# Second batch: keys and values before queries, query chunks straight into the numerator, and a later value load for the third batch

## The chip, the cores and the metric

The kernel runs on one core of a Trainium2 chip. The metric is the device time of one execution in microseconds (us). A core has a matrix engine (PE in the profile; PEld is its weight load), a vector engine (DVE), an activation engine (ACT), a general engine (POOL) and a queue engine (SP) that issues most DMAs; 16 DMA engines move the data.

## The reference

For 8 batches with 8 heads, 576 tokens and head dimension 64, a linear attention is computed, then a token-and-channel mixer on its output:

```python
def phi(x, c, s):
    r = np.maximum(x, 0.0)
    return np.concatenate([r * c, r * s], axis=-1)
q_p = phi(q, cos_w, sin_w)
k_p = phi(k, cos_w, sin_w)
kv = np.einsum('bhsf,bhsd->bhfd', k_p, v)
z = np.sum(k_p, axis=2)
num = np.einsum('bhsf,bhfd->bhsd', q_p, kv)
den = np.einsum('bhsf,bhf->bhs', q_p, z)[..., None] + 1e-06
x = num / den                      # heads side by side: 576 x 512
h = np.maximum(x.T @ w_tok1, 0.0) @ w_tok2
u = x + h.T
out = u + np.maximum(u @ w_ch1, 0.0) @ w_ch2
```

## The kernel before

Each batch's 576 tokens are cut into four chunks of 128 (`ci` 0 to 3) and a tail of 64 (`ci = R = 4`). The tails of two neighbouring batches share one 128-row tile. A batch has a **front** (class `Front`: attention and token mixer) and a **channel** part (class `Channel`: the two large matrix products). The front of batch b+1 is woven into the channel part of batch b.

The pieces of a front are: `feature`, called by `k_side` (KS) and `q_side` (QS), the ReLU features of keys and queries, a cosine and a sine half, on DVE (a sine half of the keys may go to ACT); `values` (V), the cast of the values into `v_aug`, which has a column of ones behind each head; `kv` (KV), eight matmuls of 128x65 for each chunk into one PSUM tile that collects all five chunks; `kv_out`, the copy of it to `kv_sb`, half on ACT, half on DVE; `q_trans` (QT), eight PE transposes of the query features into PSUM and a copy to `qpT`; `q_trans_dma`, the same by a transposing DMA from SP (batches 2 to 7); `num` (N), eight matmuls of `qpT` with `kv_sb`, then on DVE `den` (two small instructions) and a multiplication that gives the chunk of `x`; `mix_head` and `mix_tail`, the first token product `b_ps` and its ReLU `B`; `tok2` (T), the second token product `u_ps`, the addition on DVE that gives `u`, and a cast on ACT to `u_bf` or, for the tail, `ub_tail`; `u_trans_dma` and `tail_trans_dma`, transposing DMAs that give `uT` and `uT_tail`, which the channel part of the batch reads.

The channel part is a list of steps: 12 `c_step`s (C = 0; one 128-column block `c_ps` of the hidden layer each, four matmuls of 128x512, its ReLU `h1T` on ACT; for odd batches also four 128x128 matmuls `ct_ps` for the tails), and from step O = 12 on `o_step`s of two matmuls each (`o_ps`), whose sum with `u` goes to `o_sb` on DVE and out through SP. In the channel part of batch 0 the first twelve o steps run over chunks 0 and 1 together, four hidden blocks at a time, so that they need the three pieces of `w_ch2` one after the other.

`pieces` writes the weave as a plan of (slot, function, arguments); what stands at slot i is issued right after step i. Nothing reorders it: each engine runs its instructions in the order in which the program issues them. So the plan is the order on every engine and on SP's and POOL's DMA queues. PSUM has two pools: `ps_mm` with four one-bank buffers (`c_ps`, `ct_ps`, `o_ps`, `u_ps`, `b_ps`, half-width `qT_ps`) and `ps_at` with two two-bank buffers (`kv_ps`, `num_ps`, full-width `qT_ps`, some `u_ps`).

Batch 0 has a front of its own (`first_front`), in which nothing is woven. It ends with the first steps of channel 0. The front of batch 1 (`first` in `pieces`) is woven into channel 0, together with `tok2` of batch 0 (`u` in the plan). It has its own plan because its data arrive while it runs: `load_batch(1, ...)` waits for the first half of `w_ch1`. Later batches are loaded a batch ahead, by `load_batch` calls in the loop over steps at the end.

Of the kernel before, what the change touches and what calls it, by code (L numbers as in the profile page):

```python
# [10 lines left out]
BF16 = mybir.dt.bfloat16  # L11
# [5 lines left out]
def kernel(  # L17
# [15 lines left out]
    nc = tc.nc  # L33

    B, H, S, D = q.shape
# [4 lines left out]
    P = 128  # L40
    R = S // P
# [5 lines left out]
    NCH = D_ch // P  # L47
    HH = H // 2
# [6 lines left out]
    ORDER = (0, 1, 2, R, 3)  # L55
# [134 lines left out]
                in_=moe_w_ch1[ki * P:(ki + 2) * P, c2 * C2:(c2 + 1) * C2]  # L190
                .rearrange("(n c) d -> c n d", c=P)))
    after(w_ch1_done[0], k_done)
    def load_w_ch2(behind):
        done = [nc.gpsimd.dma_start(
            out=w_ch2[:, ki:ki + 4, :],
            in_=moe_w_ch2[ki * P:(ki + 4) * P, :].rearrange("(n t) d -> t n d", t=P))
            for ki in range(0, NCH, 4)]
        after(done[0], behind)
        return done

# [16 lines left out]
    class Front:  # L217
# [115 lines left out]
                     self.kv_ps[g][:, 0:HH * DP]  # L333
                     .rearrange("p (j d) -> p j d", d=DP)[:, :, 0:D1])

        def q_trans(self, ci, heads=(0, H), eng=nc.scalar):
            lo, hi = heads
            if hi - lo == H:
                qT_ps = ps_at.tile([P, H, P], BF16, name="qT_ps", tag="at")
            else:  # L340
                qT_ps = ps_mm.tile([P, HH, P], BF16, name="qT_ps", tag="mm")
            for h in range(lo, hi):
                nc.tensor.transpose(qT_ps[:, h - lo, :],
                                    self.q_of(ci)[:, h, :, :].rearrange("p a b -> p (a b)"), ident)
            dst = self.qpT[:, ci * H + lo:ci * H + hi, :] if ci < R else self.tail.qpT[:, lo:hi, :]
            if eng is nc.scalar:
                nc.scalar.copy(dst, qT_ps)
            else:
                nc.vector.tensor_copy(dst, qT_ps)  # L349
# [44 lines left out]
        def tok2(self, ci, pool=None, turn=True):  # L394
            res, tail = self.res, self.tail
            if ci == 0:
                res["u"] = keep.tile([P, R, Dm], F32, name="u_sb")
                if turn:
                    self.new_uT()
                    self.ub = once.tile([P, R, Dm], BF16, name="u_bf")  # L400
            if ci == R and not hasattr(tail, "u"):
                tail.new_u()
            if pool is None:
                u_ps = ps_mm.tile([P, Dm], F32, name="u_ps", tag="mm")
            else:
                u_ps = pool.tile([P, Dm], F32, name="u_ps", tag="at")
            rows = self.rows_of(ci)
            for ki in range(NT):
                nc.tensor.matmul(u_ps, w_tok2[:, ki, ci * P:(ci + 1) * P],  # L409
                                 self.B1[:, ki, :], start=(ki == 0), stop=(ki == NT - 1))  # L410
            u = res["u"][:, ci, :] if ci < R else tail.u[rows]
            nc.vector.tensor_add(u, u_ps[rows], self.x_of(ci)[rows])  # L412
            if ci == R:
                nc.scalar.copy(tail.ub[rows], u)
            elif turn:
                nc.scalar.copy(self.ub[:, ci, :], u)  # L416

        def new_uT(self):

# [41 lines left out]
        def pieces(self, b, before):  # L461


            first, odd = b == 1, b % 2 == 1
            V, KV, N = self.values, self.kv, self.num
            KS, QS, QT, T = self.k_side, self.q_side, self.q_trans, self.tok2
            C, O = 0, NCH
            if first:

                dve, every, u = nc.vector, (0, H), before.tok2  # L470
# [148 lines left out]
    def first_front(f):  # L619
# [13 lines left out]
                f.q_trans(ci, heads)  # L633
                busy(idle_ps, 1)
        f.q_side(R)
        f.q_trans(R)
        busy(idle_ps, 2)
        for ci in range(R):
            f.feature("k", ci, 0)
# [75 lines left out]


    results = [dict() for _ in range(B)]
    done = load_batch(1, "kqv", behind=w_ch1_done[1])
    w_ch2_done = load_w_ch2(done[1])
    tails = {0: tail0}  # L720
    f = Front(0, results[0], tail0)
    c = first_front(f)
    for b in range(B):
# [9 lines left out]
        for i, step in enumerate(c.steps(AHEAD if b == 0 else 0)):  # L733
# [46 lines left out]
```

## Time and profile before

| | |
|---|---|
| median of 3 runs | 276.12 us (275.65 to 276.5) |
| profiled execution | 274.87 us |
| its span in the trace | 273.1 us |
| PE busy | 260.9 us (96%) |
| DVE busy | 167.5 us (61%) |
| ACT busy | 127.0 us (47%) |
| POOL busy | 12.9 us (5%) |
| chain that ended last | PE 80%, DVE 11%, DMA 7% |

The span runs from the first to the last instruction; what the execution takes beyond it is starting and ending. Busy times of engines overlap. Matmuls are pipelined: a 128x512 matmul lasts 0.38 us in the records, and the next one starts sooner than that, so a busy PE is not a measure of how densely it is fed; the starts are.

### The profile page before, as it was taken

To read this page: it belongs to the slowest core of one execution; us is meant where nothing else is said; L and a number is where in the kernel's file an instruction comes from. 1 tells how busy PE (TensorE), PEld (TensorE's weight loads), DVE (VectorE), ACT (ScalarE), POOL (GpSimd) and SP (SyncE) were. 2 spreads that over 40 slices of the span, in tenths; PEclk is the share of its full clock that TensorE was granted. 3 is DMA by queue.
4 is the path that set the end of the run, shared out by engine and by line. 5 is a ranking of instruction groups with operands and counts; after the bars stand their busy time and mean duration, and the time that the engine had idled before them with its cause. 6 is when DMAs were issued, how large, how long until landed. Compare 5 with 4: busy or idle time off the path is not lost.

```text
span 273.1 us, 5108 instructions
## 1 busy us (share of the span) xinstructions
PE 260.9 (96%) x2029; PEld 139.3 (51%) x2050; DVE 167.5 (61%) x377; ACT 127.0 (47%) x225; POOL 12.9 (5%) x26
## 2 busy tenths in 40 slices
PE   7989979999899998999999999999999999999994
PEld 3665445446554454445654455446644455445543
DVE  6973698773876386559566387559466477720022
ACT  4955961068415184156615184338516273426500
POOL 6400240000000000000000000000000000000000
PEclk9999999999999999999999999999999999999999
DMA  7999999749985997947992969759993452170032
GB/s 224 338 270 275 333 175 276 252 98 282 272 257 183 244 212 182 333 117 234 218 305 77 264 201 253 246 149 273 157 321 105 135 95 61 41 192 21 2 99 93
DMA packets 91815, 53.68 MB, mean 197 GB/s; under 512 B 59408, under 2 KB 86928, under 8 KB 91792
## 3 DMA queue, kind: packets, MB, share of 16 engines
q1 hardware_dynamic: 88432, 49.62, 65.4%
q0 software_dynamic: 2832, 3.21, 7.0%
q10 hardware_dynamic: 528, 0.52, 0.6%
q8 instruction: 16, 0.26, 0.4%
q14 instruction: 7, 0.06, 0.1%
HBM read 35.85 MB, written 9.44 MB: 166 GB/s over the span
## 4 chain that ended last, share of the span: by engine, by line
PE 80%; DVE 11%; DMA 7%; issue 1%; DVEq 0%
PE o_ps L562 32%; PE c_ps L529 22%; PE b_ps L385 6%; PE u_ps L409 6%; DVE qp L264 4%; DMA qpT<-qp 4%; PE ct_ps L549 4%; PE num_ps L362 3%; PE kv_ps L321 3%; DVE x_sb L372 2%; DMA qt<-in_q_dram 2%; DMA uT<-u_bf 1%; DVE kp L264 1%; PE idle_ps L205 1%; PE c_ps L539 1%
## 5 line engine op out<-in xcount | busy, mean ns | idle before, releaser
L562 PE MATMUL o_ps<-w_ch,h1T 128*128 128x512 bf16 (+1 forms) x382 | 93.1, 372 | 0.6
L529 PE MATMUL c_ps<-uT,w_ch 128*128 128x512 bf16 (+2 forms) x384 | 91.9, 372 | 0.5 <-DMA uT<-u_bf 0.4
L533 ACT ACTIVATE h1T<-c_ps 128x512 bf16<-128x512 f32 x93 | 55.5, 598 | 60.2 <-PE c_ps L529 60.0
L562 PEld LDWEIGHTS <-h1T 128*128 128x128 bf16 x396 | 37.4, 98 | 39.7 <-issue 0.2
L529 PEld LDWEIGHTS <-w_ch 128*128 128x128 bf16 x384 | 33.2, 97 | 29.8 <-DMA uT<-u_bf 0.9
L567 DVE TENSOR_TENSOR o_sb<-o_ps,u_sb 128x512 f32<-128x512 f32 (+1 forms) x33 | 22.3, 674 | 37.1 <-PE o_ps L562 37.0
L412 DVE TENSOR_TENSOR u_sb<-u_ps,x_sb 128x512 f32<-128x512 f32 x32 | 22.0, 690 | 7.4 <-PE u_ps L409 6.7
L416 ACT CAST u_bf<-u_sb 128x512 bf16<-128x512 f32 x28 | 17.3, 618 | 16.9 <-DVE u_sb L412 15.2
L409 PE MATMUL u_ps<-B,w_tok 128*128 128x512 bf16 x77 | 21.9, 379 | 0.3
L390 ACT ACTIVATE B<-b_ps 128x512 bf16<-128x512 f32 x8 | 4.8, 597 | 36.0 <-PE b_ps L385 36.0
L372 DVE TENSOR_TENSOR x_sb<-num_ps,den 128x512 bf16<-128x512 f32 x28 | 19.4, 691 | 1.0
L264 DVE TENSOR_SCALAR qp<-qt,cos_t 128x512 bf16<-128x512 f32 (+1 forms) x35 | 16.7, 476 | 4.7 <-DMA qt<-in_q_dram 4.7
L549 PEld LDWEIGHTS <-w_ch 128*128 128x128 bf16 x192 | 14.0, 98 | 9.2
L385 PE MATMUL b_ps<-x_sb,w_tok 128*128 128x512 bf16 x63 | 17.7, 379 | 0.1
L264 DVE TENSOR_SCALAR kp<-kt,cos_t 128x512 bf16<-128x512 f32 x32 | 15.2, 480 | 3.9 <-DMA kt<-in_k_dram 3.9
L549 PE MATMUL ct_ps<-uT_tail,w_ch 128*128 128x128 bf16 x192 | 17.2, 219 | 0.0
L264 DVE TENSOR_SCALAR qp<-qt,sin_t 128x512 bf16<-128x512 f32 (+1 forms) x35 | 16.9, 484 | 0.0
L275 ACT CAST v_aug<-vt 128x512 bf16<-128x512 f32 (+1 forms) x28 | 15.6, 584 | 0.1
L362 PEld LDWEIGHTS <-qpT 128*128 128x128 bf16 x256 | 11.5, 98 | 7.7 <-DMA qpT<-qp 2.1
L362 PE MATMUL num_ps<-kv_sb,qpT 128*128 128x65 bf16 x256 | 13.0, 193 | 2.3 <-DMA qpT<-qp 1.5
L567 DVE TENSOR_TENSOR o_sb<-o_ps,u_tail 128x512 f32<-128x512 f32 x4 | 2.8, 692 | 19.2 <-PE o_ps L562 19.2
L321 PE MATMUL kv_ps<-v_aug,kp 128*128 128x65 bf16 x256 | 12.2, 193 | 1.0 <-DVE qpT L349 0.6
(96 smaller groups left out, 222.3 us busy)
## 6 DMA issues: line engine op xcount, KB each, us to landing
out_dram<-o_sb SPq DMA_DIRECT2D x31, 256.0 KB, 3.5
kt<-in_k_dram SPq DMA_DIRECT2D x7, 1024.0 KB, 7.2
qt<-in_q_dram SPq DMA_DIRECT2D x7, 1024.0 KB, 9.1
vt<-in_v_dram SPq DMA_DIRECT2D x7, 1024.0 KB, 6.4
w_ch<-in_moe_w_ch_dram POOLq DMA_DIRECT2D x4, 384.0 KB, 10.6
w_ch<-in_moe_w_ch_dram POOLq DMA_DIRECT2D x3, 512.0 KB, 8.2
out_dram<-o_sb SPq DMA_DIRECT2D x10, 128.0 KB, 2.3
qtt<-in_q_dram SPq DMA_DIRECT2D x8, 128.0 KB, 6.1
```

Of the source, the lines that this page charges most:

```text
L264: nc.vector.tensor_scalar(o_ap, i_ap, scalar1=w, scalar2=0.0, op0=ALU.mult, op1=ALU.max)
L321: nc.tensor.matmul(self.kv_ps[g][:, j * DP:j * DP + D1], self.k_of(ci)[:, g * HH + j, :, :] .rearrange("p a b -> p (a b)"), self.va[:, ci, ...
L362: nc.tensor.matmul(num_ps[:, g, j * DP:j * DP + D1], self.qT_of(ci, h), self.kv_sb[g][:, j, 0:D1], start=True, stop=True)
L372: nc.vector.tensor_mul(self.x_of(ci)[rows].rearrange("p (g j d) -> p g j d", g=2, j=HH), nv[:, :, :, 0:D], den.to_broadcast([rows.stop - r ...
L385: nc.tensor.matmul(self.b1_ps[mi], w, self.x_of(ci), start=(ci == ORDER[0]), stop=(ci == ORDER[-1]))
L409: nc.tensor.matmul(u_ps, w_tok2[:, ki, ci * P:(ci + 1) * P], self.B1[:, ki, :], start=(ki == 0), stop=(ki == NT - 1))
L412: nc.vector.tensor_add(u, u_ps[rows], self.x_of(ci)[rows])
L529: nc.tensor.matmul(c_ps[:, lo:hi], w_ch1[:, ki, mi * P:(mi + 1) * P], uT[:, lo // P:hi // P, ki, :], start=(ki == 0), stop=(ki == NCC - 1))
L533: nc.scalar.activation(self.h1T[:, mi, :], c_ps, AF.Relu)
L549: nc.tensor.matmul(self.ct_ps[:, mi % R, :], w_ch1[:, ki, mi * P:(mi + 1) * P], self.tail.uT[:, ki, :], start=(mi % R == 0 and ki == 0), s ...
L562: nc.tensor.matmul(o_ps, h, w_ch2[:, ki, cols], start=ki == 0, stop=ki == NCH - 1)
L567: nc.vector.tensor_add(o_sb, o_ps, u)
```

## The change

All of it is order; no arithmetic is added or dropped. (In the profile of the kernel after, lines stand a few numbers off those of before.)

- **Loads of batch 1**: keys, values, queries (before: keys, queries, values). `w_ch2`, a casting DMA in three pieces on POOL's queue, is no longer tied to the landing of batch 1's queries; it is issued at slot 8 of the plan, behind two value casts that POOL runs.
- **Front of batch 1**: key features one slot earlier (second chunk wholly on DVE); `tok2` of batch 0 at slots 5, 6, 8, 9 and 10 (before 5, 8, 11, 11, 11); values cast two on ACT, two on POOL, the tail on DVE (before four on POOL); then all of KV; only then query features and transposes, each followed at once by its `num`, spread over steps 11 to O + 7. All query transposes are copied by ACT. The token mixer starts at O + 7 (before O + 10), the second token product at O + 11 (before O + 14).
- **The tail cast** of batch 0 (`ub_tail`) becomes a function of its own at slot O + 8.
- **Batch 2**: keys and queries are loaded first (before: keys and values), the values at step O + 13 (before: queries at O + 16). Its V moves to slots 3, 3, 4, 4, 5 and its KV to 4, 5, 5, 6, 7.
- **Batches 3, 5 and 7**: query features at slots 0, 0, 1, 2 (before 1, 2, 3, 5).
- `q_trans` takes its PSUM pool as an argument.

```diff
-    def load_w_ch2(behind):
-        done = [nc.gpsimd.dma_start(
...
-        after(done[0], behind)
-        return done
+    w_ch2_done = []
+    def load_w_ch2():
+        for ki in range(0, NCH, 4):
+            w_ch2_done.append(nc.gpsimd.dma_start(
...
-        def q_trans(self, ci, heads=(0, H), eng=nc.scalar):
+        def q_trans(self, ci, heads=(0, H), eng=nc.scalar, pool=ps_mm):
             lo, hi = heads
-            if hi - lo == H:
-                qT_ps = ps_at.tile([P, H, P], BF16, name="qT_ps", tag="at")
-            else:
-                qT_ps = ps_mm.tile([P, HH, P], BF16, name="qT_ps", tag="mm")
+            qT_ps = pool.tile([P, hi - lo, P], BF16, name="qT_ps",
+                              tag="mm" if pool is ps_mm else "at")
...
-            if ci == R:
-                nc.scalar.copy(tail.ub[rows], u)
+            if turn and ci == R:
+                self.tail_cast()
             elif turn:
                 nc.scalar.copy(self.ub[:, ci, :], u)
+        def tail_cast(self):
+            nc.scalar.copy(self.tail.ub[self.rows], self.tail.u[self.rows])
...
             if first:
-                plan = [(4, KS, 0), (5, KS, 1, True), (5, u, 0, ps_at, False), (6, KS, 2, True),
-                        (7, KS, 3, True), (7, KS, R), (8, u, 1, ps_at, False), (9, QS, 0),
-                        (9, QS, 1), (10, QT, 0), (10, QS, 2), (11, QT, 1), (11, QS, 3),
-                        (11, QS, R, True), (11, u, 2, None, False), (11, QT, 2, every, dve),
-                        (11, u, 3, None, False), (11, QT, 3, every, dve), (11, QT, R, every, dve)]
-                plan += [(11, V, ci, nc.gpsimd) for ci in range(R)]
-                plan.append((11, V, R, dve))
-                plan += [(11, KV, ci) for ci in range(NSC)]
-                plan += [(11, self.kv_out), (11, u, R, None, False)]
+                plan = [(4, KS, 0), (4, KS, 1), (5, u, 0, ps_at, False), (5, KS, 2, True),
+                        (6, KS, 3, True), (6, u, 1, ps_at, False), (7, KS, R), (8, V, 0, act),
+                        (8, V, 2, pool), (8, V, 3, pool), (8, load_w_ch2),
+                        (8, u, 2, None, False), (9, V, 1, act), (9, u, 3, None, False),
+                        (10, u, R, None, False), (10, V, R, nc.vector)]
+                plan += [(11, KV, ci) for ci in range(NSC)]
+                plan += [(11, QS, 0), (11, QS, 1), (11, self.kv_out),
+                         (11, QT, 0, (0, H), act, ps_at), (11, QT, 1), (11, QS, 2), (11, QS, R),
+                         (O, QT, 2), (O, N, 0), (O, QS, 3), (O + 1, QT, R, (0, H), act, ps_at),
+                         (O + 1, N, 1), (O + 3, N, 2), (O + 3, QT, 3),
+                         (O + 5, N, R), (O + 7, N, 3), (O + 8, before.tail_cast)]
             else:
-                plan = [(C + at, V, ci, nc.scalar) for ci, at in enumerate((-1, -1, 0, 1, 2))]
+                late = b == 2
+                plan = [(C + at, V, ci, nc.scalar)
+                        for ci, at in enumerate((3, 3, 4, 4, 5) if late else (-1, -1, 0, 1, 2))]
...
-                for ci, at in zip(ORDER, (1, 2, 3, 4, 5)):
+                for ci, at in zip(ORDER, (0, 0, 1, 0, 2) if odd else (1, 2, 3, 4, 5)):
...
                 plan += [(C + at, KV, ci) for ci, at in
-                         enumerate((2, 3, 4, 5, 6) if odd else (2, 3, 4, 6, 7))]
+                         enumerate((4, 5, 5, 6, 7) if late else
+                                   (2, 3, 4, 5, 6) if odd else (2, 3, 4, 6, 7))]
...
             if first:
-                at, mix, t = (O + 1, O + 3, O + 5, O + 7, O + 9), O + 10, O + 14
+                at, mix, t = (), O + 7, O + 11
...
-    done = load_batch(1, "kqv", behind=w_ch1_done[1])
-    w_ch2_done = load_w_ch2(done[1])
+    load_batch(1, "kvq", behind=w_ch1_done[1])
...
             if b == 0 and i == NCH:
-                load_batch(2, "kv", behind=w_ch2_done[1])
-            if b == 0 and i == NCH + 16:
-                load_batch(2, "q")
+                load_batch(2, "kq", behind=w_ch2_done[1])
+            if b == 0 and i == NCH + 13:
+                load_batch(2, "v")
```

More of the change, by code (lines that the diff above doesn't have):

```diff
@@ L192 @@
     after(w_ch1_done[0], k_done)
-    def load_w_ch2(behind):
[L194 to L197, printed above, removed]
-        after(done[0], behind)
-        return done
+    w_ch2_done = []
+    def load_w_ch2():
+        for ki in range(0, NCH, 4):
+            w_ch2_done.append(nc.gpsimd.dma_start(
+                out=w_ch2[:, ki:ki + 4, :],
+                in_=moe_w_ch2[ki * P:(ki + 4) * P, :].rearrange("(n t) d -> t n d", t=P)))
     def busy(dst, times):
@@ L468, in pieces @@
             if first:
-                dve, every, u = nc.vector, (0, H), before.tok2
-                plan = [(4, KS, 0), (5, KS, 1, True), (5, u, 0, ps_at, False), (6, KS, 2, True),
-                        (7, KS, 3, True), (7, KS, R), (8, u, 1, ps_at, False), (9, QS, 0),
-                        (9, QS, 1), (10, QT, 0), (10, QS, 2), (11, QT, 1), (11, QS, 3),
-                        (11, QS, R, True), (11, u, 2, None, False), (11, QT, 2, every, dve),
-                        (11, u, 3, None, False), (11, QT, 3, every, dve), (11, QT, R, every, dve)]
@@ L476, in pieces @@
-                plan += [(11, V, ci, nc.gpsimd) for ci in range(R)]
-                plan.append((11, V, R, dve))
-                plan += [(11, KV, ci) for ci in range(NSC)]
-                plan += [(11, self.kv_out), (11, u, R, None, False)]
-            else:
-                plan = [(C + at, V, ci, nc.scalar) for ci, at in enumerate((-1, -1, 0, 1, 2))]
+                u, act, pool = before.tok2, nc.scalar, nc.gpsimd
+                plan = [(4, KS, 0), (4, KS, 1), (5, u, 0, ps_at, False), (5, KS, 2, True),
[3 more added lines that the diff above has]
+                        (10, u, R, None, False), (10, V, R, nc.vector)]
@@ L635, in first_front @@
         f.q_side(R)
-        f.q_trans(R)
+        f.q_trans(R, pool=ps_at)
         busy(idle_ps, 2)
```

## The prediction

> **What bounds the kernel now.** I read the page first, then PE's timeline stage by stage, and then the loads.
>
> ```profile
> PE 260.9 (96%) x2029; PEld 139.3 (51%) x2050; DVE 167.5 (61%) x377; ACT 127.0 (47%) x225; POOL 12.9 (5%) x26
> PEclk9999999999999999999999999999999999999999
> 108.00:256.00 148.00, 147.47 (x1061) 76.69 (x1070) 88.55 (x195) 69.06 (x123) 0.00 (x0) 1.00 0.65 178
> ```
>
> The third line is from the view of windows (length, then busy time of PE, PEld, DVE, ACT and POOL). PE is the bound. From 108 us on it is fed without a gap (147.47 of 148 us), at full clock. The change leaves every matmul in place, so it can win only what PE loses before 108 us, and lose by what it opens anywhere. Busy time hides small losses, so I take them from the starts: twelve 128x512 matmuls from 29.84 to 32.43 make 0.216 us each; four 128x128 take 0.22 us (62.68 to 62.90), so 0.056 each; eight 128x65 take 0.25 (62.90 to 63.15). What a gap holds beyond that is lost.
>
> PE's timeline in channel 0 (start, duration, then in brackets idle time and releaser):
>
> ```profile
> 29.84 2.75 PE L529 MATMUL c_ps<-uT,w_ch 128*128 128x512 bf16 x12
> 32.43 0.59 PE L409 MATMUL u_ps<-B,w_tok 128*128 128x512 bf16 x2
> ...
> 33.72 1.03 PE L529 MATMUL c_ps<-uT,w_ch 128*128 128x512 bf16 x4
> 34.98 0.62 PE L343 MATMUL qT_ps<-ident,qp 128*128 128x128 bf16 x8 [0.23 <-DVE qp L264]
> ...
> 37.99 0.38 PE L409 MATMUL u_ps<-B,w_tok 128*128 128x512 bf16 x1
> 38.81 0.62 PE L343 MATMUL qT_ps<-ident,qp 128*128 128x128 bf16 x8 [0.45 <-DVE qp L264]
> 40.65 0.61 PE L343 MATMUL qT_ps<-ident,qp_tail 128*128 128x128 bf16 x8 [1.21 <-DVE qpT L349]
> 41.85 1.15 PE L321 MATMUL kv_ps<-v_aug,kp 128*128 128x65 bf16 x32 [0.59 <-DVE qpT L349]
> ```
>
> Lost: 34.98 - 33.72 - 0.86 = 0.40; 38.81 - 37.99 - 0.22 = 0.60; 40.65 - 38.81 - 0.45 = 1.39; 41.85 - 40.65 - 0.45 = 0.75. Together 3.14 us, all waiting for DVE's query features and copies of transposes. Channels 1 and 2:
>
> ```profile
> 56.44 3.19 PE L562 MATMUL o_ps<-w_ch,h1T 128*128 128x512 bf16 x13
> 60.05 2.79 PE L529 MATMUL c_ps<-uT,w_ch 128*128 128x384 bf16 x24 [0.42 <-DMA uT<-u_bf]
> 62.68 0.39 PE L549 MATMUL ct_ps<-uT_tail,w_ch 128*128 128x128 bf16 x4
> 62.90 0.41 PE L321 MATMUL kv_ps<-v_aug,kp 128*128 128x65 bf16 x8
> 63.15 1.03 PE L529 MATMUL c_ps<-uT,w_ch 128*128 128x512 bf16 x4
> ...
> 67.76 0.39 PE L549 MATMUL ct_ps<-uT_tail,w_ch 128*128 128x128 bf16 x4
> 68.58 0.42 PE L321 MATMUL kv_ps<-v_aug,kp 128*128 128x65 bf16 x8 [0.44 <-DVE kp L264]
> ...
> 72.11 0.39 PE L549 MATMUL ct_ps<-uT_tail,w_ch 128*128 128x128 bf16 x4
> 73.20 0.42 PE L362 MATMUL num_ps<-kv_sb,qpT 128*128 128x65 bf16 x8 [0.70 <-DMA qpT<-qp]
> 103.55 1.02 PE L529 MATMUL c_ps<-uT,w_ch 128*128 128x512 bf16 x4
> 105.35 0.42 PE L362 MATMUL num_ps<-kv_sb,qpT 128*128 128x65 bf16 x8 [0.77 <-DMA qpT<-qp]
> ```
>
> Lost: 0.59 before 60.05 (14 matmuls stand there, one without a record), 0.60 at 68.58, 0.87 at 73.20, 0.94 at 105.35. So 6.1 us is the most that this change can bring.
>
> **Channel 0 after the change.** PE's order is unchanged up to c_ps 6 at 29.84. From there come 32 matmuls (c_ps 6 to 11, four `u_ps`): 6.91 us, to 36.75; then KV of all chunks, 1.25 us, to 38.0. Are their inputs there? A `num` on PE, the loads (with the time from issue to landing), POOL and DVE:
>
> ```profile
> 44.43 0.41 PE L362 MATMUL num_ps<-kv_sb,qpT 128*128 128x65 bf16 x8
> L86 SPq DMA_DIRECT2D qt<-in_q_dram x1: 1482/1482/1482, 22.6 to 22.6; - x1
> DMA to landing us min/median/max: 9.4/9.4/9.4
> L86 SPq DMA_DIRECT2D vt<-in_v_dram x1: 1457/1457/1457, 26.8 to 26.8; - x1
> DMA to landing us min/median/max: 8.7/8.7/8.7
> L194 POOL DMA_DIRECT2D w_ch<-in_moe_w_ch_dram x1: 892/892/892, 32.3 to 32.3; - x1
> DMA to landing us min/median/max: 5.9/5.9/5.9
> 35.62 2.86 POOL L277 CAST v_aug<-vt 128x512 bf16<-128x512 f32 x4 [0.94 <-DMA vt<-in_v_dram]
> 42.42 0.42 DVE L277 CAST v_aug<-vtt 64x512 bf16<-64x512 f32 x1
> 45.31 0.69 DVE L372 TENSOR_TENSOR x_sb<-num_ps,den 128x512 bf16<-128x512 f32 x1
> ```
>
> Keys first, then two loads of one size: their places are exchanged, so values land at 32.0 and queries at 35.5. POOL's two casts (0.72 each) end at 33.7, ACT's two by 35.5, so KV waits for neither. KV's last chunk needs the tail cast, which DVE reaches after the last `u` addition (PE done 35.9, sum 36.7) and ends at 37.2. So KV passes without a wait. Behind that cast DVE runs the query features, two instructions of 0.395 us a chunk (rows of batch 5 below): chunk 0 ready at 38.05, chunk 1 at 38.85, then `kv_sb`, chunk 2 at 40.05.
> - First transposes: 38.1 instead of 38.0, lost 0.1. Second: 38.9 instead of 38.55, lost 0.35.
> - First o step: `w_ch2`. POOL issues it behind its casts, at 33.7 instead of 32.3; the first piece lands 5.9 later, at 39.6. PE is there at 39.35: lost 0.3. Were this cover gone, the transposes of chunk 2 would wait for DVE until 40.05 anyway, so less than 0.3 is to be had here; a later landing counts in full. The second and third piece are needed at 44 and 47 and land, shifted by 1.4, at 42.8 and 46.5: the third has only half a microsecond to spare.
> - The second `num` needs the buffer of the first: `ps_at` has two, and the tail's `qT_ps` takes the other. The first starts at 40.55; its multiplication ends 1.55 later (45.31 + 0.69 against the `num` start at 44.43 that led to it). PE is there 1.1 later (eight 128x65, one o step, eight transposes): lost 0.45.
> The further `num` steps have 0.86 us of o matmuls or more between them and wait for nothing by this walk; the token mixer neither. 1.2 us instead of 3.14: **1.95 us gained**. Behind the waiting transposes stands all of PE's work, so these losses are whole.
>
> **Channel 1.** The mixer ends three o steps earlier in PE's order, so between its last matmul (call it U, 56.44 before) and channel 1 stand 20 matmuls, 4.32 us, instead of 14. `uT` landed at U + 3.6, so the 0.59 goes; 0.7 us is left before it would come back. Queries of batch 2 come with its keys, so DVE no longer stands in front of them with later key features behind, and the 0.60 and 0.87 go. What is late next is the values: they take the queries' place, behind the transposing DMAs of `uT` on SP.
>
> ```profile
> L86 SPq DMA_DIRECT2D qt<-in_q_dram x1: 577/577/577, 60.8 to 60.8; - x1
> DMA to landing us min/median/max: 6.0/6.0/6.0
> 62.99 0.61 ACT L275 CAST v_aug<-vt 128x512 bf16<-128x512 f32 x1
> ```
>
> Issue at U + 4.36, landing at U + 10.4, first cast done at U + 11.0. PE reaches the first KV (now slot 4) at U + 4.32 + 2.63 (60.05 to 62.68) + 0.22 + twice 1.08 (63.15 to the next `ct_ps` end) = U + 9.33. So PE stands 1.7 us at the first KV. On ACT the cast holds up the next cast and `h1T` of c_ps 4; PE's next blocks find buffers freed earlier, and the third KV waits about 0.1 for its cast. 1.8 instead of 2.06: **0.25 gained**. The bounds of this term are wide: with a landing 4.3 us after issue, sooner than any load shown, there is no stall; with the 9.4 of the first loads it is 5.1. I take 6.0, the row of a load of the same size at the same place behind the same DMAs. `qpT` of batch 2 has its input earlier than before, and the stall itself gives it time.
>
> The Trainium skill (DMA: Bandwidth & Descriptors, the anatomy of one DMA) fits 2.0 us plus bytes over 436 GB/s, for DMAs from the general engine; for 1.05 MB that is an estimate of 4.4 us, and the stall would be 0.1. The row has 6.0, since the tails' loads share the engines, and I go by the row.
>
> **Batches 3, 5 and 7.** The earlier query features bring `qpT` out earlier, and the 0.94 at 105.35 goes. But on DVE they now stand ahead of key features. Batch 5's front before (DVE, and PE beside it):
>
> ```profile
> 155.72 0.69 DVE L567 TENSOR_TENSOR o_sb<-o_ps,u_sb 128x512 f32<-128x512 f32 x1 [1.90 <-PE o_ps L562]
> 156.32 0.48 DVE L264 TENSOR_SCALAR kp<-kt,cos_t 128x512 bf16<-128x512 f32 x1
> 159.88 0.48 DVE L264 TENSOR_SCALAR kp<-kt,sin_t 128x512 bf16<-128x512 f32 x1
> 161.43 0.41 PE L321 MATMUL kv_ps<-v_aug,kp 128*128 128x65 bf16 x8
> ```
>
> DVE cannot start before 156.32, since it first adds the last o step. Its tenth instruction (159.88, so 0.395 each) ends the fourth key chunk at 160.36; KV of that chunk runs at 161.43. After the change the order is k0 k1 q0 q1 k2 q2 k3 q3: the fourth key chunk is the fourteenth instruction, 156.32 + 13 x 0.395 + 0.48 = 161.94. PE waits 0.55 us. Nothing in this stage is idle that could take it up, and the same stands in the fronts of 3, 5 and 7: **1.65 lost, 0.94 gained**.
>
> **Sum.** 1.95 + 0.25 + 0.94 - 1.65 = 1.5 us gained; I keep 1.4 for small waits that a walk by hand misses. The profiled execution took 274.87 us, so it would be 273.5; the median of the runs is 1.25 above that profile, and 276.12 - 1.4 gives **274.7**. A difference of 0.3%, 0.83 us, is about what a measurement of this kernel can tell from no change.
>
> **Rivals.**
> - *Values in time*: batch 2's values land by U + 8.7 and channel 1 loses at most 0.2. For: the load has the DMA engines to itself. Against: 6.0 is already the shortest of the large loads shown. 1.6 more: 273.1. The rule of the Trainium skill's DMA page above points here.
> - *No wait in the odd batches*: KV finds its keys ready because DVE begins earlier than 0.8 us after the channel's start. Against: the row above. 1.65 more: 273.0.
> - *`w_ch2` late*: the casting DMA starts later behind POOL's casts than 1.4 us, and the third piece misses its half microsecond as well. 1.0 less: 275.7, no difference.
> - *Values late, slower*: the values queue behind stores and transposes as the first loads did (8.7 and 9.4), at the first KV of channel 1. From a landing 7.4 us after issue the gain is gone, from 8.2 on the kernel is slower; at 8.7 to 9.4 it takes 277.4 to 278.1.
> - *Clock*: with the same late values PE stands still for 4 us or more, and restarts at a lower clock. Before, it stood 1.39 us at most and kept its clock; at the kernel's start a matmul took 0.427 us (row below), twice 0.216, for 5 us, so such a spell costs up to 2.6 us more: some 280.
>
> ```profile
> 1.38 5.12 PE L205 MATMUL idle_ps<-zeros,ident 128*128 128x512 bf16 x12 [1.38 <-POOL ident masks.py:199]
> ```
>
> The Trainium skill (TensorE: Matmul & The Clock Gate, on the clock gate) halves PE's clock after an idle window of about 3.4 us. No stall before is so long, so the trace cannot tell; at the 1.7 us forecast it would do nothing.
>
> **How the numbers follow.** The forecast has 0.45, with a range of its own from 273.9 to 275.6; of this 0.36 is faster by over 0.3% and 0.09 not to be told apart. Values in time 0.14 and no wait in the odd batches 0.08, both faster. `w_ch2` late 0.13, the same. Values late 0.17 and the clock 0.03, slower. So faster 0.58, same 0.22, slower 0.20. The range takes in the first two rivals and the values late up to a landing of 8.7: 272.8 to 277.4.
>
> **What would show it.** In the profile after: PE's first KV of channel 1 waiting for ACT's value cast, that for the load; PE's wait for DVE's keys once in channels 2, 4 and 6, half a microsecond each; no wait for `qpT` DMAs; in channel 0 waits of tenths. A first KV without a wait, or odd fronts without one, proves the sum wrong on the one side; a long wait for `w_ch2` or for the values on the other.

## The result, and the profile after

The kernel after takes **274.0 us** (median of 4 runs, 273.96 to 274.23), the kernel before, run beside it, 276.1 us (4 runs, 275.65 to 276.5): a ratio of 0.9926, 95% interval 0.9909 to 0.9943. 274.7 us had been predicted, with faster as the likeliest outcome. The profiled execution after took 273.98 us with a span of 271.8 us; before, 274.87 and 273.1.

From the page of after (busy line, granted clock), and from its view of windows, in which PE is idle for 1.14 us from 108 us on (0.53 before); the odd batches below are the reason for the difference:

```profile
PE 260.4 (96%) x2030; PEld 138.6 (51%) x2050; DVE 165.0 (61%) x376; ACT 129.7 (48%) x228; POOL 10.9 (4%) x24
PEclk9999999999999999999999999999999999999998
108.00:256.00 148.00, 146.86 (x1054) 75.84 (x1062) 86.70 (x189) 69.70 (x123) 0.00 (x0) 1.00 0.66 172
```

Busy times are almost those of before, so again only the starts tell. PE's timeline of after in channel 0 (start, duration, in brackets idle time and releaser):

```profile
36.77 1.14 PE L320 MATMUL kv_ps<-v_aug,kp 128*128 128x65 bf16 x32
37.74 0.41 PE L320 MATMUL kv_ps<-v_aug,kp_tail 128*128 128x65 bf16 x8
38.22 0.62 PE L340 MATMUL qT_ps<-ident,qp 128*128 128x128 bf16 x8
39.01 0.62 PE L340 MATMUL qT_ps<-ident,qp 128*128 128x128 bf16 x8 [0.17 <-DVE qp L263]
39.47 0.38 PE L568 MATMUL o_ps<-w_ch,h1T 128*128 128x512 bf16 x1
40.14 0.62 PE L340 MATMUL qT_ps<-ident,qp 128*128 128x128 bf16 x8 [0.29 <-DVE qp L263]
...
41.27 0.61 PE L340 MATMUL qT_ps<-ident,qp_tail 128*128 128x128 bf16 x8
42.31 0.40 PE L359 MATMUL num_ps<-kv_sb,qpT 128*128 128x65 bf16 x8 [0.44 <-DVE x_sb L369]
```

KV of all chunks passes without a wait; behind it 0.23, 0.34, 0.24 (an o step has two matmuls; one is without a record) and 0.60 us are lost. That is 1.41 us, where before lost 3.14 by the prediction's sum. Channel 1, on PE, then the values' load and their cast:

```profile
53.26 4.48 PE L568 MATMUL o_ps<-w_ch,h1T 128*128 128x512 bf16 x20
57.57 2.78 PE L535 MATMUL c_ps<-uT,w_ch 128*128 128x384 bf16 x24
60.19 0.39 PE L555 MATMUL ct_ps<-uT_tail,w_ch 128*128 128x128 bf16 x4
60.65 1.02 PE L535 MATMUL c_ps<-uT,w_ch 128*128 128x512 bf16 x4
...
62.60 0.39 PE L555 MATMUL ct_ps<-uT_tail,w_ch 128*128 128x128 bf16 x4
64.55 0.40 PE L320 MATMUL kv_ps<-v_aug,kp 128*128 128x65 bf16 x8 [1.56 <-ACT v_aug L274]
```

```profile
L86 SPq DMA_DIRECT2D vt<-in_v_dram x1: 577/577/577, 57.6 to 57.6; - x1
...
DMA to landing us min/median/max: 6.2/6.2/6.2
```

```profile
63.88 1.14 ACT L274 CAST v_aug<-vt 128x512 bf16<-128x512 f32 x2 [1.57 <-DMA vt<-in_v_dram]
```

The wait for `uT` is gone (c_ps starts where the 20 matmuls end). The values land 6.2 us after their issue; ACT waits for them, and PE for ACT: 64.55 - 62.60 - 0.22 = 1.73 us. This new wait pays for most of what channel 1 wins. A small one is at 60.65, where c_ps has no KV in front of it any more: 0.24 (ACT's first `h1T` of this channel ends at 60.6). The `kp` wait at 68.58 and the two waits for `qpT` (73.20 and 105.35) are gone. In the odd batches, PE and DVE of after at batch 5:

```profile
158.30 1.02 PE L535 MATMUL c_ps<-uT,w_ch 128*128 128x512 bf16 x4
159.63 0.42 PE L320 MATMUL kv_ps<-v_aug,kp 128*128 128x65 bf16 x8 [0.30 <-DVE kp L263]
```

```profile
159.10 0.48 DVE L263 TENSOR_SCALAR kp<-kt,sin_t 128x512 bf16<-128x512 f32 x1
```

PE stands 0.47 us here for the fourth key chunk, which DVE ends at 159.58, and 0.10 one chunk earlier. The same 0.57 stands in batches 3 and 7. All waits of after together lose 1.41 + 0.24 + 1.73 + 3 x 0.57 = 5.1 us; before lost 6.1. So the sums account for about 1.0 of the 1.25 us between the spans. Another 0.14 is a wait of before that the prediction's sum leaves out: its transposes at 37.32 start that much after the two `u_ps` matmuls from 36.75 on are through. The last 60 o matmuls start at 258.89 in before and at 257.69 in after, 1.20 apart, so hardly anything between the traces is left unnamed. The medians, however, differ by 2.1. The experiments look for the rest as well as for the share of each part.

### The profile page after: what moved, and what is told of

It is laid out like the page before. It is cut to its first block, busy times and chain, and to the rows that moved or that the text cites. A ratio compares the mean times of both kernels' runs of the same rounds, so it can differ in the third digit from the quotient of the medians.

```text
span 271.8 us, 5106 instructions
## 1 busy us (share of the span) xinstructions
PE 260.4 (96%) x2030; PEld 138.6 (51%) x2050; DVE 165.0 (61%) x376; ACT 129.7 (48%) x228; POOL 10.9 (4%) x24
## 4 chain that ended last, share of the span: by engine, by line
PE 77%; DVE 15%; DMA 4%; issue 2%; SPq 1%; ACT 0%; DVEq 0%
PE o_ps L568 32%; PE c_ps L535 19%; PE u_ps L406 6%; PE b_ps L382 6%; DVE qp L263 5%; PE ct_ps L555 4%; DVE kp L263 4%; PE num_ps L359 3%; DVE x_sb L369 3%; PE kv_ps L320 2%; DMA vt<-in_v_dram 2%; DMA qt<-in_q_dram 2%; PE idle_ps L204 1%; PE c_ps L545 1%; DVE den L367 1%
## 5 line engine op out<-in xcount | busy, mean ns | idle before, releaser
L274 ACT CAST v_aug<-vt 128x512 bf16<-128x512 f32 (+1 forms) x30 | 16.7, 586 | 1.6 <-DMA vt<-in_v_dram 1.6
L263 DVE TENSOR_SCALAR qp<-qt,cos_t 128x512 bf16<-128x512 f32 (+1 forms) x35 | 15.9, 454 | 0.7 <-DMA qt<-in_q_dram 0.7
L263 DVE TENSOR_SCALAR qp<-qt,sin_t 128x512 bf16<-128x512 f32 (+1 forms) x35 | 15.9, 454 | 0.0
```

The source lines that it names most:

```text
L263: nc.vector.tensor_scalar(o_ap, i_ap, scalar1=w, scalar2=0.0, op0=ALU.mult, op1=ALU.max)
```

## The experiments

Ratios are to the kernel before, measured beside each. "Below full clock" means executions whose mean granted clock was under 0.997; of these there is more under the first experiment. A ratio also moves with the share of such executions that before had beside it (8 of 23, 7 of 17, 7 of 12).

| kernel | median us (runs) | below full clock | ratio, 95% |
|---|---|---|---|
| after | 274.0 (4) | 0 | 0.9926 [0.9909, 0.9943] |
| before again | 275.27 (10) | 5 | 1.0011 [0.998, 1.0041] |
| odd batches as before | 272.55 (6) | 0 | 0.9883 [0.9853, 0.9912] |
| values with the keys | 277.85 (12) | 8 | 1.0048 [1.0013, 1.0084] |
| batch 1's front alone | 272.55 (6) | 0 | 0.9884 [0.9852, 0.9916] |
| before with filler | 274.15 (12) | 0 | 0.9959 [0.9941, 0.9977] |
| values two slots on | 272.51 (6) | 0 | 0.9906 [0.9877, 0.9936] |
| the same, tail in one bank | 272.01 (6) | 0 | 0.9889 [0.9864, 0.9915] |
| `w_ch2` ahead of the casts | 280.14 (6) | 5 | 1.019 [1.0162, 1.0217] |
| front alone, tail in one bank | 271.84 (6) | 0 | 0.9867 [0.9835, 0.9899] |
| front and odd batches | 273.62 (7) | 0 | 0.9926 [0.99, 0.9952] |

**The kernel before, again.** No edit; what differs from one execution to the next?

> The kernel before, unchanged, profiled a second time, because its first profiled execution (274.87 us) is 1.25 us shorter than the median of its other runs, while the kernel after was profiled at its median (274.0). Theory (the other runs of before lose more at a wait that the first profile shows smaller, one that hangs on a DMA: the transposes of queries at 73.2 and 105.4 us, or the load of batch 2's queries): the second profile is near 276 us and one or two of these waits are about 1.2 us longer in sum. Rival (the difference is no wait of PE, but something spread over the span, such as the clock or the start): the same waits to within 0.2 us and a longer span elsewhere.

Measured: of its own 10 executions 5 ran at a mean clock of 0.998 or more, with a median of 274.71 us, and 5 at 0.993 or 0.994, with 276.36. Over all 62 executions of before with a clock on record, in four groups (these 10 and the three measured beside the other kernels), 35 were at full clock (medians of the groups 274.57 to 274.98) and 27 below (275.97 to 276.55). So the rival holds, the clock. The waits for `qpT` have not grown (1.6 us in the view of waits, 1.5 in the first profile). The profiled execution here is one of the slower kind (276.19 us, span 274.4, clock 0.993). Its page, and its view of windows (length, busy time of five engines, granted clock, DMA share, GB/s):

```profile
PEclk9999997999999999999999999999999999999999
```

```profile
40.00:41.00 1.00, 0.47 (x8) 0.43 (x7) 1.00 (x3) 0.00 (x0) 0.00 (x0) 1.00 1.18 194
41.00:42.00 1.00, 0.41 (x12) 0.28 (x10) 1.00 (x3) 0.00 (x0) 0.00 (x0) 1.00 1.24 201
42.00:43.00 1.00, 1.00 (x25) 1.00 (x22) 0.69 (x2) 0.00 (x0) 0.00 (x0) 0.53 1.27 220
43.00:44.00 1.00, 1.00 (x17) 0.82 (x15) 0.00 (x0) 0.09 (x1) 0.00 (x0) 0.50 1.15 216
...
45.00:46.00 1.00, 1.00 (x9) 0.49 (x8) 0.47 (x1) 0.49 (x1) 0.00 (x0) 0.76 1.08 383
```

The clock is halved from about 42.1 to 45.5 us, right behind the two microseconds in which PE was busy 0.47 and 0.41. There PE's timeline has its waits in front of the last two transposes and of KV:

```profile
38.47 0.62 PE L343 MATMUL qT_ps<-ident,qp 128*128 128x128 bf16 x8 [0.18 <-DVE qp L264]
40.53 0.61 PE L343 MATMUL qT_ps<-ident,qp_tail 128*128 128x128 bf16 x8 [1.44 <-DVE qpT L349]
41.73 1.71 PE L321 MATMUL kv_ps<-v_aug,kp 128*128 128x65 bf16 x32 [0.59 <-DVE qpT L349]
```

The longest loses 40.53 - 38.47 - 0.45 = 1.61 us by the starts. The 32 matmuls of KV last 1.71 us instead of the 1.15 of the first profile. Executions with such a spell are 1.4 to 1.8 us longer, by the medians of the four groups. The first profile of before was one without it, although its PE stood no less; its view of windows:

```profile
40.00:41.00 1.00, 0.35 (x7) 0.35 (x7) 1.00 (x2) 0.00 (x0) 0.00 (x0) 1.00 1.21 195
41.00:42.00 1.00, 0.41 (x10) 0.24 (x8) 1.00 (x3) 0.00 (x0) 0.00 (x0) 1.00 1.26 210
```

What decides in which executions the clock falls, no run here shows.

**Before with filler.** If the cluster of waits lowers the clock, dense work in the waits must keep it up.

```diff
-                        (11, u, 3, None, False), (11, QT, 3, every, dve), (11, QT, R, every, dve)]
+                        (11, u, 3, None, False), (11, self.fill, 3), (11, QT, 3, every, dve),
+                        (11, self.fill, 6), (11, QT, R, every, dve), (11, self.fill, 3)]
```

`fill` multiplies zeros into a free one-bank buffer, nothing more.

> The kernel before, with matmuls of zeros into a spare PSUM tile in front of three waits of PE in channel 0: 3, 6 and 3 of them, 2.6 us, where PE waits 2.7. Theory (in those executions of before that show a granted clock of 0.993 in place of 0.999 and take 276.5 us in place of 274.6, the cluster of waits between 38 and 42 us makes the clock drop for 3.4 us): with PE busy in the waits no execution shows 0.993 any more, all take 274.5 to 275.2, and the median falls by up to half a microsecond. Rival (the drop has another cause, and its place there is chance): a third or more of the executions still show 0.993 and about 276.5 us.

```profile
39.32 1.46 PE L205 MATMUL fill_ps<-zeros,ident 128*128 128x512 bf16 x6
40.67 0.61 PE L343 MATMUL qT_ps<-ident,qp_tail 128*128 128x128 bf16 x8
41.12 0.81 PE L205 MATMUL fill_ps<-zeros,ident 128*128 128x512 bf16 x3
41.87 1.15 PE L321 MATMUL kv_ps<-v_aug,kp 128*128 128x65 bf16 x32
```

KV starts at 41.87 in this trace, at 41.85 in the first profile of before: the filler takes the waits' place and costs no time. None of 12 executions fell below full clock; of before, measured beside it, 7 of 17 did. The median is 274.15, so it lies with the full-clock executions of before (274.57 there) and even a little under them, which I can't explain. So the cause is shown as far as this: without PE's waits around 40 us the clock does not fall. Whether PE's standing still alone counts is open, since in that stretch PE runs nothing but transposes: in the trace with the spell, from the end of `u_ps` at 38.12 to KV at 41.73. The filler breaks up both.

**Odd batches as before.** After, with one part taken back:

```diff
-                for ci, at in zip(ORDER, (0, 0, 1, 0, 2) if odd else (1, 2, 3, 4, 5)):
+                for ci, at in zip(ORDER, (1, 2, 3, 4, 5)):
```

> The kernel after, with the query features of batches 3, 5 and 7 back in their old slots. Theory (each of the three fronts loses 0.56 us to keys that come behind queries on DVE): PE's waits for keys go, 1.7 us; the wait for the transposed queries of batch 3 comes back, about 0.9; so 273.2 us, 0.8 faster than the kernel after. Rival (the early queries are what brings the gain, and the key waits are covered elsewhere): 274.9 or slower.

Measured 272.55 us, where 273.2 had been expected: this part costs the kernel after 1.45 us. What comes back is a wait for `qpT` of batch 3, of which 0.32 us is lost by the starts (before: 0.94), because batch 2's edits already bring it forward:

```profile
102.36 0.42 PE L359 MATMUL num_ps<-kv_sb,qpT 128*128 128x65 bf16 x8 [0.16 <-DMA qpT<-qp]
```

3 x 0.57 - 0.32 = 1.4 accounts for the 1.45.

**Batch 1's front alone.** Loads and slots of batch 2 and of the odd batches as before; what is left of the change is batch 1's front and the order of the loads ahead of it.

```diff
-                late = b == 2
+                late = False
...
+                for ci, at in zip(ORDER, (1, 2, 3, 4, 5)):
...
-                load_batch(2, "kq", behind=w_ch2_done[1])
-            if b == 0 and i == NCH + 13:
-                load_batch(2, "v")
+                load_batch(2, "kv", behind=w_ch2_done[1])
+            if b == 0 and i == NCH + 16:
+                load_batch(2, "q")
```

> The new front of batch 1 alone: batch 2's loads and slots and the odd batches as in the kernel before. Theory (this front alone gains 1.75 us in channel 0 and the 0.6 of uT): 2.3 us less than before, 273.8 us; the waits of channel 1 for key features (0.6) and of batches 2 and 3 for transposed queries (0.9 each) remain. Rival (the parts need each other: batch 2's queries, loaded as late as before but with channel 1 now starting earlier against that load, cost more than before): 274.5 or slower, with the wait for key features in channel 1 grown by about a microsecond.

```profile
40.49 0.60 PE L568 MATMUL o_ps<-w_ch,h1T 128*128 128x512 bf16 x2 [0.82 <-DMA w_ch<-in_moe_w_ch_dram]
...
71.02 0.42 PE L359 MATMUL num_ps<-kv_sb,qpT 128*128 128x65 bf16 x8 [0.70 <-DMA qpT<-qp]
103.02 0.42 PE L359 MATMUL num_ps<-kv_sb,qpT 128*128 128x65 bf16 x8 [0.62 <-DMA qpT<-qp]
```

272.55 us again, the same as with batch 2's part. The 273.8 that had been expected was counted from the 276.1 of before, which holds executions below full clock; none of these six is. So the front brings the whole gain, the steady clock with it; batch 2's edits bring nothing that can be told from zero (one wait of 1.73 or 1.45 for values against waits of 0.87 and 0.79 by the starts for `qpT`), and the odd batches' edit takes 1.45 away. In this trace the front also takes away the waits for `uT` and for the keys of batch 2. And the first piece of `w_ch2` is late here: 0.99 us lost, while in the trace of after it isn't.

**Front and odd batches.** The last kernel with after's query slots in the odd batches: is their price always 1.45, or does it depend on what batch 2 has left of the wait in batch 3?

> The front of batch 1 as after and the odd batches' query features as after, batch 2 as before. Theory (my sum's price of the odd batches holds: three waits of 0.56 us for key features, and in return the wait for the transposed queries of batch 3, which is 0.79 us with the front alone, goes): 272.55 + 1.68 - 0.79 = 273.4. Rival (the odd edit costs the 1.45 us that the kernel after lost by it, whatever batch 2 does): 274.0.

Measured 273.62 us, 1.07 above the front alone (not measured side by side); 273.4 and 274.0 had been expected. It lies a little nearer to the sum of waits, which is no more than a hint. The wait of batch 3 is gone as expected, but that of batch 2 has grown in this trace, which is of the slowest of the seven executions (274.38):

```profile
71.53 0.42 PE L359 MATMUL num_ps<-kv_sb,qpT 128*128 128x65 bf16 x8 [1.29 <-DMA qpT<-qp]
```

The front's slots for batch 2 are untouched, so this wait varies by half a microsecond and more between executions or kernels, for a reason that no run here shows.

**Values with the keys.** After, with batch 2's values not loaded last:

```diff
-                load_batch(2, "kq", behind=w_ch2_done[1])
-            if b == 0 and i == NCH + 13:
-                load_batch(2, "v")
+                load_batch(2, "kqv", behind=w_ch2_done[1])
```

> The kernel after, but batch 2's values are loaded together with its keys and queries, behind them, instead of at step O + 13; the slots stay. Theory (the first KV of channel 1 waits 1.7 us for values that land 6.2 us after their issue): the values land before channel 1, the wait goes, 272.3 us. Rival (the late place of the load keeps the DMA engines free for the transposes that give uT; 1.3 MB more ahead of them makes channel 1 start later): the wait for values goes, but PE waits for uT, by up to 2 us, and the time is 274 or more.

Measured 277.85 us, and 8 of 12 executions below full clock (277.19 to 280.04; the other four 274.95 to 276.08). The wait for the values is gone, and a longer one has come in front of it, as the rival said; the view of windows shows the clock dip behind it:

```profile
53.11 4.48 PE L568 MATMUL o_ps<-w_ch,h1T 128*128 128x512 bf16 x20
60.82 3.42 PE L535 MATMUL c_ps<-uT,w_ch 128*128 128x384 bf16 x11 [3.23 <-DMA uT<-u_bf]
```

```profile
60.00:61.00 1.00, 0.18 (x1) 0.13 (x2) 1.00 (x3) 0.00 (x0) 0.00 (x0) 0.71 1.25 246
...
63.00:64.00 1.00, 1.00 (x5) 0.53 (x4) 1.00 (x4) 0.00 (x0) 0.00 (x0) 0.58 0.85 212
```

With a third large load issued ahead of them, at 48.8, the transposing DMAs of `uT` take 3.5 and 6.0 us to landing (2.4 and 3.4 in after), and PE stands 3.4 us by the starts. So the late value load in the change is what keeps `uT` in time, and its 1.7 us is the smaller of two prices. A granted clock of 0.71 is half clock for 0.58 of that microsecond: the clock fell at about 60.4, when PE had stood for 3.0 us (its 20 matmuls end at 53.11 + 20 x 0.216 = 57.43), and came back at about 63.8.

**Values two slots on.** Odd batches as before, and batch 2's V and KV two slots later, so that the load has 2.2 us more:

```diff
-                        for ci, at in enumerate((3, 3, 4, 4, 5) if late else (-1, -1, 0, 1, 2))]
+                        for ci, at in enumerate((5, 5, 6, 6, 7) if late else (-1, -1, 0, 1, 2))]
...
-                         enumerate((4, 5, 5, 6, 7) if late else
+                         enumerate((6, 6, 7, 7, 8) if late else
...
-                plan.append((C + (6 if odd else 7), self.kv_out))
+                plan.append((C + (8 if late else 6 if odd else 7), self.kv_out))
```

> The kernel after with the odd batches as before (272.55 us when run so), and batch 2's V moved on to slots 5, 5, 6, 6, 7, its KV to 6, 6, 7, 7, 8 and kv_out to 8. Theory (PE waits 1.45 us at the first KV because the values land 6.2 us after their issue, whatever stands in between): two blocks of 1.09 us more in front take the wait up, 271.1 to 271.4 us. Rival (the wait only moves: kv_out and the first num, two slots nearer, wait in its place): 272.2 or slower, with a wait of a microsecond at the first num of batch 2.

```profile
PE kv_ps L320 <- ACT v_aug L274: 0.5, 1, 0.5
...
PE num_ps L359 <- DMA qpT<-qp: 0.5, 2, 0.3
```

In the view of waits (total, times, longest) the wait for the values has shrunk to 0.5 and one for `qpT` has come in batch 2, where none was; by the starts they lose 0.68 and 0.39, where the first alone lost 1.45. 272.51 against 272.55 of the kernel without this edit (not measured side by side), where 271.1 to 271.4 had been expected: no gain that can be told from zero. Most of the wait moved.

**The tail's transposes in one bank.** The second `num` waits 0.6 us for the buffer of the first, since the tail's `qT_ps` takes the other two-bank buffer. In the last kernel, and then in batch 1's front alone:

```diff
-                         (O, QT, 2), (O, N, 0), (O, QS, 3), (O + 1, QT, R, (0, H), act, ps_at),
+                         (O, QT, 2), (O, N, 0), (O, QS, 3), (O + 1, QT, R),
```

> As the kernel with V and KV two slots on, and the tail's query transposes of batch 1 go to a ps_mm buffer instead of a ps_at one. Theory (the second num waits 0.6 us for the first num's buffer only because the tail's transposes hold the other one): that wait goes, 0.6 us, 270.6. Rival (ps_mm is as short: the transposes wait for one of its four buffers, two of which hold the o sums): the wait turns up at qT_ps instead, and the time is that of the kernel without this edit.

> The kernel after with batch 2 (its loads, value casts and KV) and the odd batches as before, so that only the front of batch 1 and the load order ahead of it are new, and with the tail's transposed queries of batch 1 in the pool of one-bank buffers, so that the second numerator step no longer waits 0.6 us for the buffer of the first. Theory: that wait was a loss of its own, nothing is late behind it, and the kernel takes 0.4 to 0.6 us less than the front alone (272.55): 272.0, some 4.1 us under the kernel before. Rival: the o steps behind the tail's transposes wait for the third piece of w_ch2 or for a one-bank buffer instead, and the time stays at 272.5.

With values two slots on 272.01 us, 0.50 under the kernel without this edit, but the two ranges overlap (271.61 to 272.65 and 271.74 to 273.17); the 270.6 that had been expected started from a base that the last experiment did not give. With the front alone **271.84 us, ratio 0.9867 [0.9835, 0.9899]**, the lowest median of the study. Its interval lies below that of after (0.9909 to 0.9943), but overlaps that of the front alone. In its timeline the second `num` follows the tail's transposes at once; the waits that are left behind it are small (this profile is of the fastest of six executions, 270.78):

```profile
41.16 0.61 PE L340 MATMUL qT_ps<-ident,qp_tail 128*128 128x128 bf16 x8
41.61 0.41 PE L359 MATMUL num_ps<-kv_sb,qpT 128*128 128x65 bf16 x8
...
57.19 2.79 PE L535 MATMUL c_ps<-uT,w_ch 128*128 128x384 bf16 x24 [0.16 <-DMA uT<-u_bf]
69.36 0.42 PE L359 MATMUL num_ps<-kv_sb,qpT 128*128 128x65 bf16 x8 [0.32 <-DMA qpT<-qp]
```

In the variant with values two slots on, the trace, of its slowest execution, shows 0.89 for `uT` at 58.12 and part of the win is gone again. That the last two medians, 272.01 and 271.84, differ is not shown, nor that 271.84 lies under the 272.55 of the front alone: none of these were measured side by side.

**`w_ch2` ahead of the casts.** After, with the casting DMA issued one slot earlier, before POOL's casts wait for the values:

```diff
-                        (6, KS, 3, True), (6, u, 1, ps_at, False), (7, KS, R), (8, V, 0, act),
-                        (8, V, 2, pool), (8, V, 3, pool), (8, load_w_ch2),
+                        (6, KS, 3, True), (6, u, 1, ps_at, False), (7, KS, R), (7, load_w_ch2), (8, V, 0, act),
+                        (8, V, 2, pool), (8, V, 3, pool),
```

> The kernel after, but w_ch2 is issued on POOL ahead of its two value casts, so that nothing holds it back. Theory (the casts, which wait for the values, are what keeps w_ch2 from running beside the loads of batch 1; without them it shares the DMA engines with keys, values and queries): the values and queries land 2 to 4 us later, PE waits at KV and at the first transposes for 2 us or more, 276 or slower. Rival (w_ch2's queue gets only what the other loads leave over, as it started when they were done in the kernel before): 274.0, nothing moves by more than a few tenths.

POOL in after, then here; and the view of waits here:

```profile
32.06 1.36 POOL L276 CAST v_aug<-vt 128x512 bf16<-128x512 f32 x2 [18.20 <-DMA vt<-in_v_dram]
33.38 2.25 POOL L196 DMA_DIRECT2D w_ch<-in_moe_w_ch_dram  x3
```

```profile
13.81 2.25 POOL L196 DMA_DIRECT2D w_ch<-in_moe_w_ch_dram  x3
39.80 1.39 POOL L276 CAST v_aug<-vt 128x512 bf16<-128x512 f32 x2 [23.74 <-DMA vt<-in_v_dram]
```

```profile
PE c_ps L535 <- ACT h1T L539: 2.9, 2, 1.5
...
PE u_ps L406 <- DVE u_sb L409: 1.2, 1, 1.2
```

280.14 us, where 276 or slower had been expected. One slot earlier in the plan is 19.6 us earlier in time (13.81 instead of 33.38), since nothing else holds POOL back. With the casting DMA under way beside it, the load of the values takes 17.8 us from issue to landing instead of 9.4, and POOL's cast starts 7.7 us later. The keys are late too: DVE's first key feature starts at 33.55 instead of 28.47. ACT's key features and then its value casts stand in front of `h1T`, DVE's key features in front of the additions that give `u`, and PE waits behind both. So the new order of batch 1's loads needs something that holds the casting DMA back, here POOL's casts, in before the tie to the queries' landing. How far forward it could go without harm was not tried.

## Why the prediction was right, and where it was not

**Channel 0** (1.95 us predicted, 1.73 measured, 1.87 with the 0.14 at 37.32). KV was to start at 36.75 and pass without a wait: 36.77, none. The first two transposes: 0.1 and 0.35 predicted, 0.23 and 0.34 measured. The second `num`: 0.45 predicted, 0.60. For `w_ch2` 0.3 had been set, with the cover that the transposes of chunk 2 would wait about as long: the first piece came in time, and chunk 2 took its place with 0.24. In the trace of the front alone the same piece was 0.99 late, so the rival "`w_ch2` late" has its place and its price in some execution of nearly the same front.

**Channel 1** (0.25 predicted, 0.09 measured). The load at the same place as the row took 6.2 us, where 6.0 was used; the first KV stands 1.73, where 1.7 was forecast; the waits for `uT`, keys and `qpT` of batch 2 went as said. The Trainium skill (DMA: Bandwidth & Descriptors, the anatomy of one DMA) would have made this load 4.4 us by its fit, an estimate; the 6.2 of the trace decides. Not seen: KV in front of c_ps 4 had covered 0.25 us in which ACT has to empty a buffer; with KV moved on, 0.24 of wait appears there. It was a cover that the walk didn't name.

**Odd batches** (1.65 lost and 0.94 gained predicted). Three times 0.57 measured, by the mechanism told: DVE takes the keys later. The wait of batch 3 went too. That this part of the change is a loss was forecast and is shown by taking it back. What the sum overlooked is that batch 2's edits alone had brought that wait down to 0.32: in the whole change the odd slots had 0.3 left to win and lost 1.7.

**From trace to time, the step that failed.** The sum from trace to trace was 1.4 us and the spans differ by 1.25, but two steps behind it were wrong, in opposite directions.
- *Outside the span*: the new kernels take 2.15 us beyond their span (all nine that have the new front, 2.12 to 2.17 in the median), before and before with filler 1.8. 0.35 us is given back there; the sum had taken this time as fixed. What it is was not tried and stays open.
- *"The median of the runs is 1.25 above that profile, and 276.12 - 1.4 gives 274.7"*: this offset was carried over to the changed kernel. It does not belong to the measurement, it belongs to before: the offset is mostly the clock dip, 1.4 to 1.8 us, which 27 of 62 executions of before contain, its first profile by chance doesn't, and none of after's 4 does. The sentence that the change "can win only what PE loses before 108 us" leaves this out. After's profile lies at its own median (273.98 and 274.0). By their times, the four runs of before beside after (275.65 to 276.5) are mostly executions with a dip; their clock is not on record. Against the full-clock median of the largest group, 274.63 (15 executions, not measured beside after), the difference is only 0.6 us; so an estimated 1.5 of the 2.1 us that were measured are put down to the dip.

So the predicted 273.5 for the profiled execution was 0.5 too low, and the offset 1.25 too high, and the sum came out 0.7 above the result. The waits were forecast to tenths by the right mechanism; that the time came out near as well, and that the gain was so clear of noise, is in good part luck, since most of the measured gain has a cause that the sum doesn't hold.

**The rivals.** *Values in time* and *no wait in the odd batches* did not happen (1.73 and 0.57). *Values late, slower* did not: 6.2 is below the 7.4 from which the gain would have gone. *Clock* was set down for a stall of 4 us that the change might open, with the words that before "stood 1.39 us at most and kept its clock". One trace can't carry that sentence. The clock was at stake the other way round: the change takes a dip away. Where a long stall does open, as with the values loaded with the keys (3.4 us by the starts for `uT`), the dip does come, in 8 of 12 executions. The Trainium skill (TensorE: Matmul & The Clock Gate, on the clock gate) speaks of an idle window of about 3.4 us before the clock is halved. With the values loaded with the keys the clock fell when PE had stood for 3.0 us. At the end of the kernels, where PE has nothing left to do, it fell after 2.2 us in after (PE done at 268.25, granted clock 0.73 in the microsecond from 270 on) and was still full after 3.5 us with the odd batches as before (266.46 to 270). So less than 3.4 us of standing can be enough, and more can pass without a fall; the measurement decides. In the dip of before no single wait was above 1.61 us, and PE was busy 0.47 and 0.41 in the two microseconds ahead of it; but between 38.12 and 41.73 it ran only transposes, and no run here tells whether these count as work for the clock. So that dip alone does not tell how long PE must stand.

## What to carry to other kernels

A cluster of PE waits can cost more than its idle time: look at the granted clock of every execution, not of one profile, and before an offset between profile and median is carried over, find out what it consists of. An early place in a queue is paid for by whoever stood there: query features ahead of key features cost three times 0.57 us to save a wait of 0.3, and batch 2's values, moved to the end, exchanged waits of 0.87 and 0.79 us for one of 1.7. Try the parts of a change one by one, since here one part of three brought all of the gain and another gave back 1.45 us.

## What the runs showed of the hardware

- The granted clock of PE fell to half for some 3.4 us in both traces that show it in mid-kernel. With the values loaded with the keys it fell after PE had stood for 3.0 us, at the end of after following 2.2 us; with the odd batches as before it was still full 3.5 us after PE's last work. In before it fell behind two microseconds of PE busy 0.47 and 0.41, with no wait above 1.61 us, but with nothing except transposes in 3.6 us. In the first profile of before, with 0.35 and 0.41 at the same place, it held.
- Executions of before below full clock were 27 of 62, and took 1.4 to 1.8 us more; with the same waits filled with zero matmuls there were 0 of 12.
- With a casting DMA of three pieces under way beside it, a 1 MB load took 17.8 us to landing instead of 9.4 (POOL's cast at 39.80 instead of 32.06).
- With one more 1 MB load issued ahead of them, the two transposing DMAs of `uT` took 3.5 and 6.0 us to landing instead of 2.4 and 3.4.
